# A decode step of cached attention and a gated MLP: part of one weight block by a transfer of its own, and scratch products ahead of half the V tiles

## The chip, the cores and the metric

The kernel runs on one core of a Trainium2 chip. That core has TensorE (PE, with its weight loads as PEld), VectorE (DVE), ScalarE (ACT), GpSimd (POOL) and SyncE (SP), and sixteen DMA engines that the queues of SP and ACT share. The metric is the device time of one execution in microseconds; the lower the better. All data are fp32.

## The reference

Eight tokens (B = 8) of width D = 512, one new position each. With xn = layernorm(x), the result is x + s * silu(y):

```python
q = (xn @ wq)                       # 32 heads of 128, grouped on 8 KV heads (REP = 4)
scores = q . k_cache * 128**-0.5    # cache of 4096 positions per token and KV head
s = softmax(scores) . v_cache @ wo  # wo is 4096 x 512
z = gelu(xn @ w_in)                 # 512 x 1792
z1, z2 = z[..., :896], layernorm(z[..., 896:])
y = (z1 * (w_sp * z2 + b_sp)) @ w_out   # w_out is 896 x 512
```

The K and V caches are 134 MB each, wq and wo 8.4 MB each, w_in and w_out 5.5 MB together; each byte is read once.

## The kernel before

Three SBUF slots of 64 KB per partition (`slot_a`, `slot_b`, `slot_c`; 8.4 MB each) take everything that is read. All transfers but the output's are issued from SP, in program order. In `prologue`, wq goes to slot b, then x, then the MLP's rows `w_mlp` to slot c (per partition: w_in, w_out as NB = 7 blocks of 128 rows, and a few scalars), then the first K tile to slot a. When q has been computed, the second K tile goes to slot b.

The MLP is computed in the prologue too. Its activations lie in four row groups of 32 partitions (`G` = 4, `R` = 32), 256 features in each of the first three and 128 in the last; they are transposed to `hT`, and the loop at L207 to L211 multiplies them with the seven blocks of w_out. Blocks 2g and 2g + 1 add up in row group g of the PSUM tile `pw`; block 6, the last, is alone in row group 3.

Then come eight KV heads, one after the other, each with four tiles: K for tokens 0 to 3 (slot a), K for tokens 4 to 7 (slot b), V for tokens 0 to 3 (slot c), V for tokens 4 to 7 (slot b). `Heads.loads` is SP's program: each transfer waits on PE's count for the products that free its slot. `head_products` is PE's program, one body that a loop on PE's own sequencer runs eight times; DVE and ACT have theirs written out (`head_sides`). PE waits for a tile's landing (`landed_a`, `landed_b`, `landed_c`) and for tokens from DVE (`take`), so its instructions stand in a fixed order: scores from both K tiles (L353), three small products for the softmax over row groups (L357 to L361), products of `pT` with the first V tile into `o_ps[0]` and with the second into `o_ps[1]` (L372), then two small products into `po` (L382), with two scratch products between them (L379) whose result nobody reads.

After the last head, `last_products` multiplies the heads' outputs with wo, which SP loads in six pieces into slot a (`WO_PIECES`; column 2m and 2m + 1 belong to product m). Products 0 to 27 are folded (L408, into `sc` and `o_ps`, copied out by DVE and ACT, and added up by `pick`, L430); products 28 to 31 go directly to `acc` (L417), two of them before L430 and two behind it. The last piece of wo holds one column. `last_sides` multiplies with the gate, adds x, and ACT stores the result.

Of the kernel before, what the change touches and what calls it, by code (L numbers as in the profile page):

```python
# [10 lines left out]
P = 128  # L11
B, D = 8, 512
HKV, REP, S, DH = 8, 4, 4096, 128
NK = D // P
G = 4
J = S // (G * P)
R = 32
FH = 896
FQ = 256
NB = FH // P  # L20
# [8 lines left out]
FOLDED = HKV * REP - REP  # L29
AHEAD = FOLDED + 2  # L30
HD = 256
N_IN, N_OUT = NK * 2 * FH, NB * D
N_MLP = N_IN + N_OUT + R
STEPS = 8
WARM = 384


class Chip:
# [49 lines left out]
        self.same_all = self.same.rearrange("p g r -> p (g r)")  # L88


def prologue(tc, t, x, w_mlp, wq, k0, k1, landed_a, landed_b):

    nc = tc.nc
    slot_a, slot_b, slot_c = t.slots
    nc.sync.dma_start(slot_b, wq)
    wq_sb = slot_b.rearrange("p (k n) -> p k n", k=NK)
    w_in_sb = slot_c[:, :N_IN].rearrange("p (k n) -> p k n", k=NK)
    w_out_sb = slot_c[:, N_IN:N_IN + N_OUT].rearrange("p (j d) -> p j d", j=NB)
    side_sb = slot_c[:, N_IN + N_OUT:N_MLP]
    x_sb = slot_c[:B, N_MLP + P:N_MLP + P + D]  # L100
    xn = slot_c[:B, N_MLP + P + D:N_MLP + P + 2 * D]
    nc.sync.dma_start(x_sb, x)
    nc.sync.dma_start(slot_c[:, :N_MLP], w_mlp)
    first = nc.sync.dma_start(slot_a, k0).then_inc(landed_a, 16)
    tc.no_tile_sem_insts.add(first.ins.name)

# [21 lines left out]
    def scratch(*shape):  # L128
        turn[0] ^= 1
        n = 1  # L130
        for s in shape[1:]:
            n *= s
        return t.scr[turn[0]][:shape[0], :n]
# [11 lines left out]
    for quad in range(HKV // G):  # L145
        pq = scratch(P, REP * DH)
        for k in range(NK):
            for g in range(G):
                lo = (quad * G + g) * REP * DH
                nc.tensor.matmul(pq[R * g:R * (g + 1), :], t.xnT[:, k, :], wq_sb[:, k, lo:lo + REP * DH],  # L150
                                 start=(k == 0), stop=(k == NK - 1))
# [12 lines left out]
    z, u_sb = zu[:, 0], zu[:, 1]  # L164
    rest = t.pT.rearrange("p j b g r -> p (j b g r)")
    hT, y_sb = rest[:, :2 * P].rearrange("p (a s) -> p a s", a=2), rest[:, D:]
# [36 lines left out]
    for a in range(2):  # L203
        th = scratch(P, P)
        nc.tensor.transpose(th, u_sb[:, 1, a * P:(a + 1) * P], t.ident)
        nc.vector.tensor_copy(hT[:, a, :], th)
    pw = scratch(P, D)  # L207
    for j in range(NB):
        g, a = divmod(j, 2)
        nc.tensor.matmul(pw[R * g:R * (g + 1), :], hT[:, a, R * g:R * (g + 1)], w_out_sb[:, j, :],  # L210
                         start=(a == 0), stop=(a == 1 or j == NB - 1))  # L211
    nc.vector.tensor_copy(y_sb, pw)
    py = scratch(P, W)
    for g in range(G):
# [3 lines left out]
    e = t.o_all.rearrange("p g d -> p (g d)")[:, :W]  # L218
# [9 lines left out]


class Heads:  # L230

# [109 lines left out]
    def head_products(self):  # L343
        nc, t, step = self.nc, self.t, lambda mm: mm.then_inc(self.pe, 1)
        slot_a, slot_b, slot_c = t.slots
        for half, (slot, landed) in enumerate(((slot_a, self.landed_a), (slot_b, self.landed_b))):
            self.take(landed, 16)
            k_sb = slot.rearrange("p (i c g s) -> p i c g s", i=HALF, c=2, g=G)
            for i in range(HALF):
                b = half * HALF + i  # L350
                for c in range(2):
                    for g in range(G):
                        mm = nc.tensor.matmul(t.sc[R * g:R * (g + 1), c, :], t.q[:, b * R:(b + 1) * R],  # L353
                                              k_sb[:, i, c, g, :], start=(b == 0), stop=(b == B - 1))
            step(mm)
        self.take(self.token, 1)
        step(nc.tensor.transpose(t.scr[0][:1, :P], t.nm, t.ident))  # L357
        self.take(self.token, 1)
        step(nc.tensor.transpose(t.scr[1][:, :1], t.full.rearrange("b g r -> b (g r)"), t.ident[:1, :1]))
        self.take(self.token, 1)  # L360
        step(nc.tensor.matmul(t.scr[1][:, 1:2], t.same_all, t.wl, start=True, stop=True))  # L361
        self.take(self.token, 1)
        pT = t.pT.rearrange("p j b g r -> p j b (g r)")
        for half, (slot, landed) in enumerate(((slot_c, self.landed_c), (slot_b, self.landed_b))):
            if half:
                self.take(self.token, 1)
            self.take(landed, 16)
            v_sb = slot.rearrange("p (i j e) -> p i j e", i=HALF, j=J)
            of = t.o_ps[half].rearrange("p g d -> p (g d)")
            for j in range(J):  # L370
                for i in range(HALF):
                    mm = nc.tensor.matmul(of[R * i:R * i + G * REP, :], pT[:, j, half * HALF + i],  # L372
                                          v_sb[:, i, j], start=(j == 0), stop=(j == J - 1))
            step(mm)
        n = HALF * REP
        for half in range(2):
            if half:
                for _ in range(2):
                    nc.tensor.matmul(t.scr[1][:, :WARM], t.ident, pT.rearrange("p j b x -> p (j b x)")[:, :WARM],  # L379
                                     start=True, stop=True)  # L380
            self.take(self.token, 1)
            mm = nc.tensor.matmul(t.po[:, half * n:(half + 1) * n], t.o_sb[half],  # L382
                                  t.fold.rearrange("p i r -> p (i r)"), start=True, stop=True)
        step(mm)
# [53 lines left out]
        step(mm)  # L438


def gqa_gmlp_decode(nc, x, kT, v, wq, wo, w_mlp, x_rows, out):
    t = Chip(nc)
    landed_a, landed_b, stored = (nc.alloc_semaphore(s) for s in ("landed_a", "landed_b", "stored"))
    with tile.TileContext(nc) as tc:
        prologue(tc, t, x, w_mlp, wq, kT[0, 0], kT[0, 1], landed_a, landed_b)
    heads = Heads(nc, t, landed_a, landed_b, stored)
    heads.loads(kT, v, wo, x_rows)
    for h in range(HKV):
        heads.head_sides(h)
    heads.last_sides(out)  # L450
    nc.sync.wait_ge(stored, 16).then_inc(stored, -16)
    with nc.tensor.Fori(0, HKV):
        heads.head_products()
    heads.last_products()
# [39 lines left out]
```

## Time and profile before

| what | us |
|---|---|
| median of 3 runs (lowest to highest) | 678.75 (678.7 to 679.01) |
| profiled execution, its own time | 679.39 |
| its span, first to last instruction | 678.1 |
| PE busy | 351.0 |
| PE weight loads busy | 102.7 |
| DVE busy | 80.7 |
| mean granted clock of PE | 0.748 |
| data queue of SP: bytes, share of sixteen engines | 290.79 MB, 99.1% |

Busy time is the time in which an engine worked on anything; a group of instructions is given by its line, its engine and the tiles it writes and reads. A matmul of fp32 data shows as two records. The granted clock is the share of TensorE's full clock that the chip allowed. The time ahead of an instruction in which its engine did nothing is given with what ended it. "PEq" is PE's own sequencer, which carries out PE's waits for landings and tokens, so that a wait for a transfer reads as a wait on PEq.

### The profile page before, as it was taken

How to read it: one execution, taken by the hardware profiler on the slowest of the kernel's cores; microseconds unless marked ns; L12 is line 12 of the kernel's file. 1: busy time of each engine (PE TensorE's matmuls, PEld its weight loads, DVE VectorE, ACT ScalarE, POOL GpSimd, SP SyncE). 2: the span in 40 equal slices, each digit the busy share in tenths (PEclk: the TensorE clock that was granted, in tenths of full speed). 3: DMA queues.
4: the chain of work that ended last, by engine and by line, in shares of the span. 5: the costliest groups of instructions: out<-in, count | busy, mean ns of one | idle time of the engine just before them, and what ended most of it. 6: DMA issues, size and time to landing. Idle time of an engine off the chain costs nothing. (4 is left out here: it accounts for less than half of the span.)

```text
span 678.1 us, 5431 instructions
## 1 busy us (share of the span) xinstructions
PE 351.0 (52%) x2480; PEld 102.7 (15%) x2480; DVE 80.7 (12%) x156; ACT 13.8 (2%) x28; POOL 2.8 (0%) x15
## 2 busy tenths in 40 slices
PE   0446743545565444456555444655645454655548
PEld 0112210111121111111111110111111111211104
DVE  0142021102110021101100021101101021100111
ACT  0010000000000000000000000000000000000000
POOL 1000000000000000000000000000000000000000
PEclk9986766778767677877766677887666678877659
DMA  9999999999999999999999999999999999999996
GB/s 383 439 433 434 434 433 433 434 433 433 433 433 433 433 433 433 437 437 437 445 437 433 437 437 433 441 437 433 433 433 433 433 433 433 433 433 433 433 414 287
DMA packets 6070, 290.90 MB, mean 429 GB/s; under 512 B 936, under 2 KB 1064, under 8 KB 1456
## 3 DMA queue, kind: packets, MB, share of 16 engines
q1 hardware_dynamic: 5920, 290.79, 99.1%
q8 instruction: 4, 0.07, 0.0%
q10 hardware_dynamic: 144, 0.03, 0.0%
q14 instruction: 2, 0.02, 0.0%
HBM read 290.78 MB, written 0.03 MB: 429 GB/s over the span
## 5 line engine op out<-in xcount | busy, mean ns | idle before, releaser
L372 PE MATMUL o_ps<-slot_b,pT 128*16 128x512 f32 x512 | 74.9, 751 | 81.0 <-PEq L341 81.0
L353 PE MATMUL sc<-slot_b,q 128*32 128x512 f32 x512 | 74.4, 746 | 73.5 <-PEq L341 73.5
L353 PE MATMUL sc<-slot_a,q 128*32 128x512 f32 x512 | 75.5, 756 | 56.2 <-PEq L341 56.2
L372 PE MATMUL o_ps<-slot_c,pT 128*16 128x512 f32 x512 | 73.9, 742 | 47.9 <-PEq L341 47.9
L258 DVE TENSOR_REDUCE nm<-sc 128x1 f32<-128x1024 f32 x8 | 9.8, 1225 | 277.0 <-PE sc L353 277.0
L258 DVE TENSOR_TENSOR o_all<-o_ps,diag 128x512 f32<-128x512 f32 x16 | 11.1, 692 | 243.4 <-PE o_ps L372 243.4
L353 PEld LDWEIGHTS sc<-slot_b,q 128*32 128x32 f32 x512 | 20.4, 134 | 127.5 <-issue 127.5
L372 PEld LDWEIGHTS o_ps<-slot_b,pT 128*16 128x16 f32 x512 | 17.6, 114 | 138.4 <-issue 138.4
L353 PEld LDWEIGHTS sc<-slot_a,q 128*32 128x32 f32 x512 | 20.7, 135 | 104.7 <-issue 104.7
L372 PEld LDWEIGHTS o_ps<-slot_c,pT 128*16 128x16 f32 x512 | 17.4, 114 | 97.7 <-issue 97.7
L289 ACT ACTIVATE p<-sc,nm 128x1024 f32<-128x1024 f32 x8 | 8.9, 1114 | 554.4 <-DVE nm L258 554.4
L258 DVE TENSOR_REDUCE o_sb<-o_all 128x128 f32<-128x512 f32 x16 | 16.4, 1025 | 0.5
L142 PE MATMUL scr<-ident,slot_c 8*128 8x8 f32 x4 | 0.6, 255 | 25.2 <-DVE slot_c L139 25.2
L379 PE MATMUL scr<-pT,ident 128*128 128x384 f32 x32 | 12.3, 507 | 0.0
L258 DVE STREAM_TRANSPOSE pT<-p 128x1024 f32<-128x1024 f32 x8 | 10.0, 1245 | 0.3
L150 PE MATMUL scr<-slot_b,xnT 128*32 128x512 f32 x64 | 9.0, 717 | 0.3 <-DVE xnT L143 0.3
L357 PE MATMUL scr<-ident,nm 128*1 128x128 f32 x8 | 2.2, 269 | 11.9 <-PEq L341 11.9
L382 PE MATMUL po<-fold,o_sb 128*128 128x16 f32 x32 | 6.1, 266 | 2.5 <-PEq L341 2.5
L361 PE MATMUL scr<-wl,same 128*128 128x1 f32 x16 | 3.6, 297 | 6.6 <-PEq L341 6.6
L382 PEld LDWEIGHTS po<-fold,o_sb 128*128 128x128 f32 x32 | 4.8, 188 | 14.0 <-issue 14.0
L258 DVE TENSOR_SCALAR p<-p,w,wl 128x1024 f32<-128x1024 f32 x8 | 6.5, 813 | 0.3
L379 PEld LDWEIGHTS scr<-pT,ident 128*128 128x128 f32 x32 | 5.5, 191 | 2.1
(92 smaller groups left out, 77.9 us busy)
## 6 DMA issues: line engine op xcount, KB each, us to landing
slot_c<-in_w_mlp SPq DMA_DIRECT2D x1, 5392.0 KB, 33.8
slot_a<-in_wo SPq DMA_DIRECT2D x1, 4608.0 KB, 40.1
slot_a<-in_wo SPq DMA_DIRECT2D x1, 2048.0 KB, 44.5
slot_a<-in_wo SPq DMA_DIRECT2D x2, 512.0 KB, 45.7
slot_a<-in_wo SPq DMA_DIRECT2D x1, 384.0 KB, 46.7
slot_a<-in_kT SPq DMA_DIRECT2D x8, 48.1
slot_b<-in_kT SPq DMA_DIRECT2D x8, 29.2
slot_c<-in_v SPq DMA_DIRECT2D x8, 48.1
```

The lines of the kernel that those rows point to most:

```text
L142: nc.tensor.transpose(pt[:, k * B:(k + 1) * B], xn[:, k * P:(k + 1) * P], t.ident[:B, :B])
L150: nc.tensor.matmul(pq[R * g:R * (g + 1), :], t.xnT[:, k, :], wq_sb[:, k, lo:lo + REP * DH], start=(k == 0), stop=(k == NK - 1))
L258: make(*args, **kw).then_inc(self.dve, 1)
L289: nc.scalar.activation(p, t.sc.rearrange("p c s -> p (c s)"), AF.Exp, bias=t.nm, accum_out=t.l).then_inc(self.act, 1)
L353: mm = nc.tensor.matmul(t.sc[R * g:R * (g + 1), c, :], t.q[:, b * R:(b + 1) * R], k_sb[:, i, c, g, :], start=(b == 0), stop=(b == B - 1))
L357: step(nc.tensor.transpose(t.scr[0][:1, :P], t.nm, t.ident))
L361: step(nc.tensor.matmul(t.scr[1][:, 1:2], t.same_all, t.wl, start=True, stop=True))
L372: mm = nc.tensor.matmul(of[R * i:R * i + G * REP, :], pT[:, j, half * HALF + i], v_sb[:, i, j], start=(j == 0), stop=(j == J - 1))
L379: nc.tensor.matmul(t.scr[1][:, :WARM], t.ident, pT.rearrange("p j b x -> p (j b x)")[:, :WARM], start=True, stop=True)
L382: mm = nc.tensor.matmul(t.po[:, half * n:(half + 1) * n], t.o_sb[half], t.fold.rearrange("p i r -> p (i r)"), start=True, stop=True)
```

## The change

Two parts.

First, w_out's last block. Its 128 rows no longer lie in the MLP's rows as one more block. Rows 64 to 127 are folded: their two halves of 256 columns lie on partitions 0 to 63 and 64 to 127, so that each MLP row gets 256 numbers (1,024 bytes) shorter. Rows 0 to 63 come by a transfer of their own, `w_lane`: five groups of 13 rows of 2,048 bytes (65 rows, the last of them zeros; in memory each group is followed by a row that is not read, so that five is an axis of its own). In the computation, the one product with block 6 becomes three: one of 512 columns over 64 rows, and two of 256 columns with operands `h_half`, in which half of the rows are zero. For `h_half` there is one more transpose, a memset and two copies.

Second, in every head, PE computes nine scratch products of 128 x 512 (identity times part of `pT`, into the scratch bank, read by nobody) behind the first V tile's products and ahead of the wait for the second V tile. They are a loop on PE's sequencer inside the loop over heads.

```diff
+WHOLE = NB - 1
+LANES, ROWS = 5, 13
+N_IN, N_OUT = NK * 2 * FH, WHOLE * D + D // 2
+AHEAD_OF_V = 9
...
     nc.sync.dma_start(slot_c[:, :N_MLP], w_mlp)
+    spare = N_MLP + P + 2 * D
+    w_lane_sb = slot_c[:LANES * ROWS, spare:spare + D]
+    h_half = slot_c[:, spare + D:spare + D + 2 * R].rearrange("p (e s) -> p e s", e=2)
+    nc.sync.dma_start(w_lane_sb, w_lane[:, :ROWS])
     first = nc.sync.dma_start(slot_a, k0).then_inc(landed_a, 16)
...
+    last_rows, low, high = slice((G - 1) * R, P), slice(0, P // 2), slice(P // 2, P)
+    tl = scratch(P // 2, R)
+    nc.tensor.transpose(tl, u_sb[last_rows, 1, P // 2:P], t.ident[last_rows, last_rows])
+    nc.vector.memset(h_half, 0.0)
+    nc.vector.tensor_copy(h_half[low, 0], tl)
+    nc.vector.tensor_copy(h_half[high, 1], hT[high, 0, last_rows])
     pw = scratch(P, D)
-    for j in range(NB):
+    for j in range(WHOLE):
         g, a = divmod(j, 2)
         nc.tensor.matmul(pw[R * g:R * (g + 1), :], hT[:, a, R * g:R * (g + 1)], w_out_sb[:, j, :],
-                         start=(a == 0), stop=(a == 1 or j == NB - 1))
+                         start=(a == 0), stop=(a == 1))
+    pl = pw[last_rows, :]
+    nc.tensor.matmul(pl, hT[low, 0, last_rows], w_lane_sb[low, :], start=True, stop=False)
+    for e in range(2):
+        nc.tensor.matmul(pl[:, e * (D // 2):(e + 1) * (D // 2)], h_half[:, e], w_half_sb, start=False, stop=(e == 1))
...
         for half, (slot, landed) in enumerate(((slot_c, self.landed_c), (slot_b, self.landed_b))):
             if half:
+                flat = t.pT.rearrange("p j b g r -> p (j b g r)")
+                with nc.tensor.Fori(0, AHEAD_OF_V):
+                    nc.tensor.matmul(t.scr[1], t.ident, flat[:, :512], start=True, stop=True)
                 self.take(self.token, 1)
             self.take(landed, 16)
...
+    w_lane = np.zeros((LANES * ROWS, D), np.float32)
+    w_lane[:P // 2] = w_out[-1, :P // 2]
+    w_lane = np.pad(w_lane.reshape(LANES, ROWS, D), ((0, 0), (0, 1), (0, 0)))
```

How the instructions stand. On PE, in one head, before (from the softmax's last small product to the end of the loop over heads):

```order
L361 MATMUL scr<-wl,same 128x1
L372 MATMUL o_ps<-slot_c,pT 16x512 x32
L372 MATMUL o_ps<-slot_b,pT 16x512 x32
L382 MATMUL po<-fold,o_sb 128x16
L379 MATMUL scr<-pT,ident 128x384 x2
L382 MATMUL po<-fold,o_sb 128x16
```

And now (lines are those of the changed kernel):

```order
L381 MATMUL scr<-wl,same 128x1
L395 MATMUL o_ps<-slot_c,pT 16x512 x32
L387 UNCONDITIONAL_BRANCH
L388 MATMUL scr<-pT,ident 128x512
L387 REGISTER_ALU
L387 COMPARE_AND_BRANCH
L395 MATMUL o_ps<-slot_b,pT 16x512 x32
L405 MATMUL po<-fold,o_sb 128x16
L402 MATMUL scr<-pT,ident 128x384 x2
L405 MATMUL po<-fold,o_sb 128x16
```

One product and its loop's branches stand between the two V tiles' products; the product is run nine times in each of eight heads.

On SP, the prologue's transfers, before:

```order
L95 DMA slot_b<-in_wq 128x16384
L102 DMA slot_c<-in_x 8x512
L103 DMA slot_c<-in_w_mlp 128x10784
L104 DMA slot_a<-in_kT 128x16384
L160 DMA slot_b<-in_kT 128x16384
```

And now:

```order
L98 DMA slot_b<-in_wq 128x16384
L106 DMA slot_c<-in_x 8x512
L107 DMA slot_c<-in_w_mlp 128x10528
L111 DMA slot_c<-in_w_lane 65x1x512
L112 DMA slot_a<-in_kT 128x16384
L168 DMA slot_b<-in_kT 128x16384
```

The MLP's rows are 256 numbers shorter, and a transfer of 65 rows stands between them and the first K tile.

More of the change, by code (lines that the diff above doesn't have):

```diff
@@ L31 @@
 HD = 256
-N_IN, N_OUT = NK * 2 * FH, NB * D
+WHOLE = NB - 1
+LANES, ROWS = 5, 13
+N_IN, N_OUT = NK * 2 * FH, WHOLE * D + D // 2
 N_MLP = N_IN + N_OUT + R
@@ L88, in __init__, with prologue @@
         self.same_all = self.same.rearrange("p g r -> p (g r)")
-def prologue(tc, t, x, w_mlp, wq, k0, k1, landed_a, landed_b):
+def prologue(tc, t, x, w_mlp, w_lane, wq, k0, k1, landed_a, landed_b):
     nc = tc.nc
@@ L97, in prologue @@
     w_in_sb = slot_c[:, :N_IN].rearrange("p (k n) -> p k n", k=NK)
-    w_out_sb = slot_c[:, N_IN:N_IN + N_OUT].rearrange("p (j d) -> p j d", j=NB)
+    w_out_sb = slot_c[:, N_IN:N_IN + WHOLE * D].rearrange("p (j d) -> p j d", j=WHOLE)
+    w_half_sb = slot_c[:, N_IN + WHOLE * D:N_IN + N_OUT]
     side_sb = slot_c[:, N_IN + N_OUT:N_MLP]
@@ L438, in last_products, with gqa_gmlp_decode @@
         step(mm)
-def gqa_gmlp_decode(nc, x, kT, v, wq, wo, w_mlp, x_rows, out):
+def gqa_gmlp_decode(nc, x, kT, v, wq, wo, w_mlp, w_lane, x_rows, out):
     t = Chip(nc)
@@ L444, in gqa_gmlp_decode @@
     with tile.TileContext(nc) as tc:
-        prologue(tc, t, x, w_mlp, wq, kT[0, 0], kT[0, 1], landed_a, landed_b)
+        prologue(tc, t, x, w_mlp, w_lane, wq, kT[0, 0], kT[0, 1], landed_a, landed_b)
     heads = Heads(nc, t, landed_a, landed_b, stored)
@@ L481 @@
             c(B_w_in).reshape(NK, P, 2 * FH).transpose(1, 0, 2).reshape(P, NK * 2 * FH),
-            w_out.transpose(1, 0, 2).reshape(P, NB * D),
+            w_out[:-1].transpose(1, 0, 2).reshape(P, WHOLE * D),
+            w_out[-1, P // 2:].reshape(P // 2, 2, D // 2).transpose(1, 0, 2).reshape(P, D // 2),
             side], axis=1),
+        "w_lane": w_lane,
         "x_rows": x_rows.reshape(P, W),
```

## The prediction

> **What bounds the kernel now.** I read the page first, for the transfers, then busy time by stretch, then the tail.
>
> ```profile
> span 678.1 us, 5431 instructions
> DMA  9999999999999999999999999999999999999996
> q1 hardware_dynamic: 5920, 290.79, 99.1%
> ```
>
> The DMA engines are busy from end to end: 290.79 MB on one queue fill 99.1% of sixteen engines' span. What TensorE (PE) does in mid-kernel costs no time. By stretch (columns: length, busy time of each engine with counts, granted clock, DMA share, GB/s):
>
> ```profile
> 75.00:575.00 500.00, 260.89 (x1740) 73.43 (x1740) 54.58 (x95) 9.86 (x21) 0.00 (x0) 0.73 1.00 434
> 672.50:673.00 0.50, 0.50 (x14) 0.21 (x6) 0.00 (x0) 0.00 (x0) 0.00 (x0) 1.00 0.53 176
> 673.00:673.50 0.50, 0.50 (x14) 0.25 (x10) 0.00 (x0) 0.00 (x0) 0.00 (x0) 1.00 0.32 113
> 673.50:674.00 0.50, 0.50 (x16) 0.30 (x10) 0.00 (x0) 0.00 (x0) 0.00 (x0) 1.00 0.29 90
> 674.00:674.50 0.50, 0.50 (x30) 0.39 (x27) 0.17 (x1) 0.11 (x1) 0.00 (x0) 1.00 0.14 35
> ```
>
> At 434 GB/s one engine of sixteen moves 27.1 GB/s. The engines do not end together. From 673.0 on the share is 0.32 of sixteen, that is five engines; the other eleven ran dry near 672.7, the five go on to about 674.3, some 1.5 us longer. The likely reason is in the queue rows: code comes in over the same engines. The first row is the whole run's, the second that of 672 to 675 us:
>
> ```profile
> q8 instruction: 4, 0.07, 0.0%
> q8 instruction: 1, 0.02, 1.8%
> ```
>
> Four blocks of some 16 KB and two smaller ones, each on some engine, hold up that engine's data. No view names single engines. Following the packets by hand, each starting where its engine's last one ended, I find the fetches on five engines; the transfer of x uses eight engines, and only one of the five late ones is among these eight.
>
> The tail, in order of time (start, length, engine, line; in brackets the idle time before):
>
> ```profile
> 636.02 9.32 PE L372 MATMUL o_ps<-slot_c,pT 128*16 128x512 f32 x64 [6.64 <-PEq L341]
> 655.32 9.91 PE L372 MATMUL o_ps<-slot_b,pT 128*16 128x512 f32 x64 [9.98 <-PEq L341]
> 665.41 1.54 PE L379 MATMUL scr<-pT,ident 128*128 128x384 f32 x4
> 667.64 0.62 PE L408 MATMUL sc<-slot_a,oT 128*8 128x256 f32 x8
> 673.91 0.38 PE L408 MATMUL o_ps<-slot_a,oT 128*8 128x256 f32 x1
> 674.39 0.37 ACT L330 COPY part_sb<-o_ps 128x256 f32<-128x256 f32 x1 [45.76 <-PE o_ps L408]
> 675.12 0.42 PE L430 MATMUL acc<-part_sb,pick 128*16 128x64 f32 x16 [0.38 <-PEq L341]
> 675.34 0.64 PE L417 MATMUL acc<-slot_a,oT_last 128*16 128x64 f32 x32
> 676.04 0.23 DVE L258 TENSOR_TENSOR gate<-acc,gate 128x64 f32<-128x64 f32 x1 [1.28 <-PE acc L417]
> ```
>
> PE runs without a break from 667.64 to 674.29: the folded products with wo (L408), the copies, `pick` (L430), the last direct products (L417). The weights they use arrive as follows (issue times, then KB and us from issue to landing; the six issues start 0.475 us apart):
>
> ```profile
> 625.90 2.80 SPq L279 DMA_DIRECT2D slot_a<-in_wo  x6
> slot_a<-in_wo SPq DMA_DIRECT2D x1, 4608.0 KB, 40.1
> slot_a<-in_wo SPq DMA_DIRECT2D x1, 2048.0 KB, 44.5
> slot_a<-in_wo SPq DMA_DIRECT2D x1, 384.0 KB, 46.7
> slot_a<-in_wo SPq DMA_DIRECT2D x1, 128.0 KB, 46.4
> ```
>
> So the first piece lands at 666.0, the second at 626.4 + 44.5 = 670.9, the fifth at 627.8 + 46.7 = 674.5, the sixth at 628.3 + 46.4 = 674.7. The last L417 group needs the fifth piece, and starts at 675.34, 0.8 us after it. In this execution the last 0.7 us thus belong to PE's chain, which started when the last V tile arrived (655.32); behind it, closely, stands the landing of wo.
>
> **The change, part by part.**
>
> *Fewer MLP bytes per row.* Each of the 128 rows gets 1,024 bytes shorter; an engine carries eight rows, 8,192 B, which at 27.1 GB/s is 0.30 us. Every later landing on an engine outside the five groups moves up by 0.30 us.
>
> *The transfer of five groups.* 65 rows of 2,048 B in five groups of 13. If each group goes to one engine, that engine gets 26,624 B, 0.98 us, less 0.30: it ends 0.68 us later. An early engine has 1.5 us to give, so it stays ahead of the late five. Bounds: all 65 rows on one engine would be 4.9 us there, spread over sixteen 0.3 us. I take five, as the access pattern is cut. The Trainium skill (DMA: Bandwidth & Descriptors, "Why a DMA increments its semaphore by 16 and not by 1") says that a transfer runs on the largest number of engines up to 16 that divides both slowest dimensions, the lowest-numbered ones; by it 5 and 65 give five engines, and they lie inside the eight of x. No view of this case shows it yet. [...]
>
> *Prologue work.* One more transpose, a memset, two small copies, and three products for one. The rows it resembles, and its cover:
>
> ```profile
> 53.73 0.50 DVE L206 COPY pT<-scr 128x128 f32<-128x128 f32 x2 [0.63 <-PE scr L205]
> 54.07 3.43 PE L210 MATMUL scr<-slot_c,pT 128*32 128x512 f32 x14 [0.17 <-DVE pT L206]
> 75.41 9.75 PE L353 MATMUL sc<-slot_b,q 128*32 128x512 f32 x64 [4.02 <-PEq L341]
> ```
>
> Seven products took 3.43 us, so two more are 1 us, at worst 1.7 us one after another; with copies and a transpose below 1 us together, 3 us at most. Everything behind waits for the second K tile, before which PE idles 4.02 us, so this costs nothing; without that cover it would be up to 3 us on the scores, still hidden by the DMA queue, in which a whole tile is waiting. One more issue on SP ahead of the first K tile lies under the transfer of wq:
>
> ```profile
> slot_b<-in_wq SPq DMA_DIRECT2D x1, 21.9
> ```
>
> *Nine scratch products ahead of each second V tile.* They stand in PE's queue behind the first V tile's products (end 645.34) and ahead of two waits; the second tile's products are queued behind them. Clock and pace (the last two rows count o_ps alone):
>
> ```profile
> 644.00:647.46 3.46, 1.34 (x16) 0.12 (x4) 1.71 (x2) 0.00 (x0) 0.00 (x0) 1.00 0.83 360
> 647.46:654.29 6.83, 0.00 (x0) 0.00 (x0) 0.00 (x0) 0.00 (x0) 0.00 (x0) 0.50 0.94 408
> 655.32:661.11 5.79, 5.79 (x28) 1.30 (x32) 0.00 (x0) 0.00 (x0) 0.50 1.03 446
> 661.11:665.23 4.12, 4.12 (x40) 0.95 (x32) 0.00 (x0) 0.00 (x0) 1.00 0.94 404
> ```
>
> The clock is full when the first tile's products end, falls to half at 647.46 after a stretch that was 39% busy, and the second tile runs its first 5.79 us at half clock (0.207 us per record against 0.103). A scratch product: L379 took 1.54 us for two of 384 columns, 1.03 us scaled to 512, the upper end; the lower is two records at a quarter of the array's four-wide pace, 8 x 0.103 = 0.82 us. Nine take 7.4 to 9.2 us, and end at 652.8 to 654.6, before the tile (655.32 - 0.30 = 655.0). PE then idles 0.4 to 2.2 us; the clock should hold, and the tile takes 64 x 0.103 = 6.6, with its end some 6.9 us, instead of 9.91. PE would reach L408 3.3 us earlier, at 664.3. In seven of eight heads this buys nothing, as DMA is the bound.
>
> *The tail now.* What is late next is wo. Its first piece lands at 665.7. I add 0.1 us for a wait's release (bounds 0, and the 0.36 us from the ACT copy's end, 674.76, to L430). L408's 56 products go at 0.114 us each (667.64 to 673.91): 36 of them from 665.8 to 669.9; the other 20 from the second piece, 670.7, to 673.0, with the tail of the last 673.3. From L408's end to L430 it took 0.83 us (674.29 to 675.12), L430's head start is 0.22: 674.35. The fifth piece is there at 674.5 - 0.3 + 0.1 = 674.3 too. L417 ends at 675.0 instead of 675.98: 1.0 us less.
>
> **Against the median.** The sum is made on the profiled execution, 679.39 us (678.1 and 1.29 around it), giving 678.4. The runs' median is 678.75, 0.64 lower. One reason is in the page:
>
> ```profile
> L372 PE MATMUL o_ps<-slot_b,pT 128*16 128x512 f32 x64 | 9.9, 788 | 10.0 <-PEq L341 10.0
> L372 PE MATMUL o_ps<-slot_b,pT 128*16 128x512 f32 x512 | 74.9, 751 | 81.0 <-PEq L341 81.0
> ```
>
> The last V tile took 9.9 us here, the mean of eight heads is 74.9 / 8 = 9.36: where the clock's step falls varies. In a usual execution PE's chain ends 0.55 us earlier, at 675.43, and wo's landing allows 675.25. There the change buys 675.43 - 675.0 = 0.45 us. I predict 678.3 us.
>
> **Rivals.**
>
> *A. A late engine is among the five.* Then it ends 0.68 us later, not 0.30 earlier. If it is the last of all, wo's fifth piece lands at 675.2, L417 ends at 675.95, and a usual execution becomes 0.5 us slower, 679.25; if it ends 0.3 us before the last, 678.95. For it: one late engine lies among x's eight. Against it: three of these eight are outside the five. It decides once that engine's lag plus 0.68 passes the others' less 0.30.
>
> *B. The clock falls in the gap after the scratch products.* A gap of up to 2.2 us leaves a 3.4 us stretch no more than 36% busy, and 39% was too little at 647. Then only the 0.30 us of landing stay, for PE's chain too: 678.45.
>
> *C. The scratch products overrun the tile*, the slower side. From 645.34 to 655.0 are 9.7 us, and L408 can slip by 1.5 more, so it decides from 1.24 us a product. At half clock they take 1.64 to 2.06, 14.8 to 18.5 in all: the tile starts 5.1 to 8.8 us late, saves 3.0, and the kernel takes 681 to 685. Against it: the clock is full when they start. The Trainium skill (Runtime: NRT & Kernel Launch, "Instruction fetch mechanics") says that a taken branch out of a two-block window stalls on a fetch. As a mechanism here: 1.8% of sixteen engines over 3 us is 0.86 us a fetch, with nine turns 7.8 us more, the same overrun. The trace speaks against it: all eight turns of the long head loop, with four q8 blocks in the run.
>
> *D. The change does not do what it says*: the groups land on one engine, which ends 4.6 us later, 3.1 us past the others' old end: 681.7.
>
> **How the numbers follow.** Forecast 0.5 (678.3, its own range 677.6 to 678.7), A 0.28, B 0.12, C 0.06, D 0.04. A measurement of this kernel can tell about 0.2%, 1.36 us, from no change: 677.4 and 680.1. The forecast, A and B lie inside; beyond the lower bound lies the forecast's edge, where executions like the profiled one, with its 1.0 us, are the usual ones or more than five engines gain: 0.1. C and D are slower: 0.1. The range that holds 8 in 10 takes in A with its bounds: 677.5 to 679.4.
>
> **What would show it.** Five engines' stretch in the changed profile: DMA share 0.6 near 673, with five engines of an extra step between the early and the late. The last wo landing earlier by 0.3 us: right; later by 0.4 or more: A. The clock at 1.00 from the first V tile to the tail and the second V tile near 6.9 us: right; 9 us and more: B. PE idle before L408 and again before its last 20 products: wo is the bound. A second V tile that starts after 655.5 is C. It would be wrong as a whole if the DMA queue had gaps in mid-kernel.

## The result, and the profile after

| | before | changed |
|---|---|---|
| median, 23 executions each | 678.98 us | 680.61 us |
| lowest | 678.37 us | 679.66 us |
| ratio, 95% interval | | 1.0038 [1.0026, 1.0050] |

The changed kernel is slower by 0.38%; 678.3 us had been forecast, with a range up to 679.4. Three of its executions (755.9 to 777.5 us; in the profiled one, 774.82 us, the core reads 376 GB/s over the span) are left out of the ratio, as are fourteen at 690 to 778 us of e1, e2, e6, e13 and e14, the kernels below with five groups of 10 or 13 rows; no other kernel here had one. The other twenty fall in two lots: sixteen from 679.66 to 681.47, mean 680.36, and four from 685.5 to 686.7. The sixteen stand 1.38 us above the median of before. The four, 5.8 us above the sixteen, add 4/20 of that, 1.16 us, to the mean. So there are two losses of about equal size to explain.

The profile below is of a second run of the changed kernel (`e1_again`), whose profiled execution took 681.61 us. From its page, the span, the DMA slices and the data queue:

```profile
span 679.6 us, 5886 instructions
...
DMA  9999999999999999999999999999999999999996
...
q1 hardware_dynamic: 5990, 290.79, 99.0%
```

The bytes are the same to two decimals and the queue is as full: 131,072 bytes left the MLP's rows, 133,120 came by the new transfer. The busy time of engines by stretch (columns as in the prediction; DMA share and GB/s last):

```profile
75.00:575.00 500.00, 305.85 (x1865) 96.10 (x1866) 54.66 (x95) 9.86 (x21) 0.00 (x0) 0.78 1.00 434
672.50:673.00 0.50, 0.50 (x16) 0.24 (x11) 0.00 (x0) 0.00 (x0) 0.00 (x0) 1.00 0.92 324
673.00:673.50 0.50, 0.50 (x18) 0.26 (x10) 0.00 (x0) 0.00 (x0) 0.00 (x0) 1.00 0.56 211
673.50:674.00 0.50, 0.50 (x16) 0.31 (x12) 0.00 (x0) 0.00 (x0) 0.00 (x0) 1.00 0.54 191
674.00:674.50 0.50, 0.50 (x14) 0.24 (x7) 0.00 (x0) 0.00 (x0) 0.00 (x0) 1.00 0.29 92
674.50:675.00 0.50, 0.50 (x14) 0.23 (x9) 0.00 (x0) 0.00 (x0) 0.00 (x0) 1.00 0.06 25
675.00:676.00 1.00, 1.00 (x42) 0.70 (x36) 0.15 (x1) 0.09 (x1) 0.00 (x0) 1.00 0.05 16
```

In mid-kernel it reads 434 GB/s, as before. At the end the sixteen engines stop in three steps. Near 673.2 the share is 0.56, nine engines; by 674.5 it is 0.06, a single engine, and this one works on until after 675.5. Before, the last five were done by 674.5. What the single engine carries is the end of wo (issue of its six pieces on SP, one every 0.475 us; then KB and time to landing, the second to fourth and the sixth piece between them):

```profile
626.92 2.80 SPq L299 DMA_DIRECT2D slot_a<-in_wo  x6
slot_a<-in_wo SPq DMA_DIRECT2D x1, 2048.0 KB, 44.8
slot_a<-in_wo SPq DMA_DIRECT2D x1, 384.0 KB, 46.8
slot_a<-in_wo SPq DMA_DIRECT2D x1, 128.0 KB, 46.7
```

The fifth piece (384 KB) lands at 626.92 + 4 x 0.475 + 46.8 = 675.6, where it was 674.5 before. PE's tail, in order of time:

```profile
637.30 9.07 PE L395 MATMUL o_ps<-slot_c,pT 128*16 128x512 f32 x64 [6.90 <-PEq L361]
646.30 7.99 PE L388 MATMUL scr<-pT,ident 128*128 128x512 f32 x18
656.62 7.06 PE L395 MATMUL o_ps<-slot_b,pT 128*16 128x512 f32 x64 [2.33 <-PEq L361]
667.48 0.62 PE L431 MATMUL sc<-slot_a,oT 128*8 128x256 f32 x8 [1.42 <-PEq L361]
669.68 1.11 PE L431 MATMUL sc<-slot_a,oT 128*8 128x256 f32 x8
675.63 0.62 PE L440 MATMUL acc<-slot_a,oT_last 128*16 128x64 f32 x28
676.64 0.42 PE L453 MATMUL acc<-part_sb,pick 128*16 128x64 f32 x16 [0.38 <-PEq L361]
676.86 0.64 PE L440 MATMUL acc<-slot_a,oT_last 128*16 128x64 f32 x32
```

The scratch products (L388) do what was meant: the second V tile's products take 7.06 us instead of 9.91. PE then waits 1.42 us for wo. The direct products (L440) start at 675.63, the moment the fifth piece is there, and the last ends at 677.50, 1.52 us later than before (675.98). The clock on the way:

```profile
646.30:654.29 7.99, 7.99 (x22) 3.33 (x18) 1.74 (x2) 0.00 (x0) 0.00 (x0) 1.00 0.87 378
654.29:656.62 2.33, 0.01 (x1) 0.04 (x2) 0.00 (x0) 0.00 (x0) 0.00 (x0) 1.00 1.10 475
656.62:663.68 7.06, 7.06 (x65) 2.03 (x65) 0.00 (x0) 0.00 (x0) 0.00 (x0) 1.00 0.97 418
666.00:668.00 2.00, 0.58 (x13) 0.35 (x16) 0.29 (x2) 0.00 (x0) 0.00 (x0) 1.00 0.95 410
669.00:672.00 3.00, 3.00 (x36) 1.35 (x30) 0.00 (x0) 0.00 (x0) 0.00 (x0) 0.50 0.97 398
```

It holds at 1.00 through the second V tile, and falls to half for 3.4 microseconds in the products with wo: the stall that the scratch products removed has moved to the wait for wo, and the clock fell there.

### The profile page after: what moved, and what is told of

Read it like the earlier page. It is cut to its first block, busy times and chain, and to the rows that moved or that the text cites. A ratio compares the mean times of both kernels' runs of the same rounds, so it can differ in the third digit from the quotient of the medians.

```text
span 773.2 us, 5886 instructions
## 1 busy us (share of the span) xinstructions
PE 412.6 (53%) x2629; PEld 129.6 (17%) x2629; DVE 81.3 (11%) x159; ACT 13.8 (2%) x28; POOL 2.8 (0%) x15
## 5 line engine op out<-in xcount | busy, mean ns | idle before, releaser
L373 PE MATMUL sc<-slot_b,q 128*32 128x512 f32 x512 | 72.2, 728 | 98.0 <-PEq L361 98.0
L395 PE MATMUL o_ps<-slot_c,pT 128*16 128x512 f32 x512 | 76.0, 760 | 76.0 <-PEq L361 76.0
L395 PE MATMUL o_ps<-slot_b,pT 128*16 128x512 f32 x512 | 72.0, 725 | 37.4 <-PEq L361 37.4
L388 PE MATMUL scr<-pT,ident 128*128 128x512 f32 x144 | 63.9, 598 | 0.0
L388 PEld LDWEIGHTS scr<-pT,ident 128*128 128x128 f32 x144 | 26.7, 190 | 37.4 <-issue 37.4
```

The lines of the kernel that those rows point to most:

```text
L388: nc.tensor.matmul(t.scr[1], t.ident, flat[:, :512], start=True, stop=True)
```

## The experiments

Theory A is rival A of the prediction: the engine that ends last is among the five, and every row that it is given puts off the last landing of wo. Theory P came late: five engines that run about half a 64 KB packet behind the others make all reads slower. All ratios are to the kernel before, run on the same chip. Landing times given per engine, and the length of single packets, are read from the trace's own records of landings and packets; no view shows them.

### The two halves alone

The changed kernel a second time:

> The changed kernel once more, for a profile beside those of its parts. Both theories: 680 to 681 us. Theory L (the lanes: five DMA engines that run 1 us behind the others disturb the reads of all) expects a rate under 434 GB/s in mid-kernel. Theory S (the scratch products: PE's inner loop delays PE, or its own code fetches, and with it the tail) expects 434 GB/s in mid-kernel and a last V tile that starts late.

1.0032 [1.0014, 1.0050]; its compared executions took 679.75, 680.12, 681.61 and 683.43 us. The landings of wo's sixth piece come at 672.9 to 673.2 on seven engines, at 674.1 to 674.7 on eight, and at 675.97 on one. The new transfer's own semaphore rises five times, so it does run on five engines.

The block's split and transfer, without the scratch products:

```diff
-                flat = t.pT.rearrange("p j b g r -> p (j b g r)")
-                with nc.tensor.Fori(0, AHEAD_OF_V):
-                    nc.tensor.matmul(t.scr[1], t.ident, flat[:, :512], start=True, stop=True)
```

> The changed block of w_out alone, no scratch products. Theory L: all of the loss is here, 680 to 681 us, mid-kernel rate under 434 GB/s. Theory S: 678.4 to 679.3 us, by rival A or the forecast's DMA term, 434 GB/s.

1.0042 [1.0019, 1.0065]; seven executions lie from 679.81 to 680.72, two at 686.25 and 686.65. This part alone brings the whole loss, both lots of it. By stretch:

```profile
673.00:673.50 0.50, 0.50 (x16) 0.26 (x11) 0.00 (x0) 0.00 (x0) 0.00 (x0) 1.00 0.59 228
675.00:675.50 0.50, 0.50 (x28) 0.39 (x23) 0.01 (x1) 0.00 (x0) 0.00 (x0) 1.00 0.06 25
675.50:676.00 0.50, 0.39 (x27) 0.22 (x14) 0.41 (x1) 0.37 (x1) 0.00 (x0) 1.00 0.07 23
```

Nine engines at 673, a single one from 675 to 676, as in the whole change.

The scratch products alone, on the kernel before:

```diff
+AHEAD_OF_V = 9
...
             if half:
+                flat = t.pT.rearrange("p j b g r -> p (j b g r)")
+                with nc.tensor.Fori(0, AHEAD_OF_V):
+                    nc.tensor.matmul(t.scr[1], t.ident, flat[:, :512], start=True, stop=True)
                 self.take(self.token, 1)
```

> The nine scratch products alone. Theory L: not slower than before, 678.3 to 679.0 us, and the second V tile takes 6.9 us. Theory S: all of the loss is here, 680 us or more, and the last V tile starts more than 0.3 us after its landing.

1.0021 [0.9998, 1.0045]: ten executions from 678.64 to 680.89 and one at 688.31. No gain, and a spread that before does not have (678.44 to 679.48). The execution at 688.31 had a mean granted clock of 0.629, the other ten 0.796 to 0.811. In the profiled one (678.81 us) the gap behind the scratch products cost the clock:

```profile
644.50 7.99 PE L369 MATMUL scr<-pT,ident 128*128 128x512 f32 x18
655.36 8.76 PE L376 MATMUL o_ps<-slot_b,pT 128*16 128x512 f32 x64 [2.87 <-PEq L342]
655.36:659.50 4.14, 4.14 (x24) 1.14 (x28) 0.00 (x0) 0.00 (x0) 0.00 (x0) 0.59 0.99 427
659.50:664.10 4.60, 4.60 (x45) 1.24 (x37) 0.00 (x0) 0.00 (x0) 0.00 (x0) 1.00 0.91 393
```

After 2.87 us of idleness the clock is mostly at half up to 659.5: rival B, in this execution. The sixth piece of wo lands at 674.75, against 674.68 before, so the scratch products do not move the transfers.

### How many engines, how many rows

Here the scratch loop is out, and only the cut of the transfer changes. If theory A holds, the loss must follow the rows per engine, and vanish when each of sixteen engines gets four (the 8 KB that its shorter MLP rows saved).

```diff
-LANES, ROWS = 5, 13
+LANES, ROWS = 16, 4      # e4_spread16
+LANES, ROWS = 4, 16      # e5_lanes4
+LANES, ROWS = 8, 8       # e9_lanes8
+LANES, ROWS = 5, 25      # e10_rows25: 61 of the 125 rows are zeros
```

> As e2_lanes, but the 64 rows come in sixteen groups of four, so that each of sixteen engines carries as many bytes as before. Theory L: 678.7 to 679.2 us, as before, since no engine is set back against the others. Theory S: the same, as there are no scratch products. If it is at 680 us or more, the cause is neither the lag nor the scratch products, but the extra transfer itself, its 2 KB rows or the prologue's added work.

> As e2_lanes, but four groups of 16 rows instead of five of 13. Theory A (rival A: one of the five engines that take the groups is itself a late one, so the last landing moves back by about 1.3 us): if that engine is the fifth, wo's last landing comes 0.3 us earlier than before and the time is 678.4 to 678.7 us; if it is one of the first four, each takes 32 KB instead of 26 KB and the time is 680.2 to 681 us, 0.2 above e2_lanes. Theory N (no engine is special; the extra small rows slow all): 680 to 681 us with five or more engines late at the end together.

> As e2_lanes, but eight groups of 8 rows: eight engines carry 16 KB each. Theory A (the engine that fetches DVE's code is among those that take groups, and ends last): the last landing goes with the rows on that engine; 13 rows moved it by +1.3 us, so a row costs 0.12 us with the 0.30 us taken off once, and 8 rows give +0.65: 679.5 us. Theory N (not the rows on one engine but an extra transfer cut finer than sixteen): 680.5 us as e2_lanes.

> As e2_lanes, but five groups of 25 rows, 12 of them idle zeros: the five engines are set back by about one whole 64 KB packet (2.42 us) instead of half of one. Theory A: +2.7 us on the last landing, 681.5 us. Theory P (where the values lie more than 1.5 us above the lowest of a kernel, the reads of two groups of engines half a packet apart disturb each other): the values keep within 1.5 us. Without P: scattered upward as e2_lanes.

| run | rows per engine | sixth piece of wo, last landing | executions, us | ratio |
|---|---|---|---|---|
| before | 0 | 674.68 | 678.4 to 680.2 | |
| e4_spread16 | 4 | 674.79 | 678.70 to 679.86 (11) | 1.0006 [0.9997, 1.0015] |
| e9_lanes8 | 8 | 675.23 | 679.10 to 680.46 (10) | 1.0010 [1.0001, 1.0019] |
| e1, e2 | 13 | 675.97, 676.31 | see above | 1.0032, 1.0042 |
| e5_lanes4 | 16 | 676.47 | 680.33 to 682.70 (6) | 1.0034 [1.0022, 1.0046] |
| e10_rows25 | 25 | 677.57 | 681.40 to 681.81 (5) | 1.0039 [1.0026, 1.0052] |

The landing follows the rows, and with it the time. From e4's 674.79 to e10's 677.57 it is 2.78 us for 21 rows, 0.13 us a row. The ends of the DMA show it, first e4's and then e10's:

```profile
674.00:674.50 0.50, 0.43 (x32) 0.28 (x24) 0.00 (x0) 0.00 (x0) 0.00 (x0) 1.00 0.23 72
674.50:675.00 0.50, 0.50 (x44) 0.50 (x39) 0.00 (x0) 0.00 (x0) 0.00 (x0) 1.00 0.02 5
```

```profile
675.50:676.00 0.50, 0.50 (x16) 0.24 (x8) 0.00 (x0) 0.00 (x0) 0.00 (x0) 1.00 0.12 37
676.50:677.00 0.50, 0.50 (x32) 0.36 (x29) 0.29 (x1) 0.30 (x1) 0.00 (x0) 1.00 0.06 25
```

With four rows each the last engine is done by about 674.6; with 25 on five of them one engine alone still reads at 676.5 to 677. The same split of the block, with all its extra products in the prologue, costs at most 0.15% when its rows are spread: the prologue's work is not the loss.

### The rows without their use, and which engine is late

An idle transfer of zeros, five groups of seven rows, on the kernel before; nothing reads it:

```diff
     nc.sync.dma_start(slot_c[:, :N_MLP], w_mlp)
+    spare = N_MLP + P + 2 * D
+    nc.sync.dma_start(slot_c[:5 * 7, spare:spare + D], idle[:, :7])
```

> The kernel before, and one transfer of five groups of 7 rows of zeros that nothing uses; w_out's block stays in the MLP's rows. Theory A: the last landing +0.84 us (7 rows at 0.12), 679.7 us, with no change to anything that is computed. If it is as before, 678.9 us, the loss of e2_lanes comes from the computation or the MLP's rows.

1.0032 [1.0008, 1.0056]: ten executions from 679.07 to 681.21, median of all 679.64, and two at 686.63 and 687.39. The last landing is at 675.36. The transfer alone, with no work behind it, brings both lots of the loss.

Three small transfers, whose packets differ in length, mark the engines:

```diff
+    for n, cols in ((4, 448), (3, 384), (2, 320)):
+        nc.sync.dma_start(slot_c[:n, spare:spare + cols], idle[:n, :cols])
+        spare += D
```

> The kernel before, with three small transfers of 4, 3 and 2 rows of different lengths that nothing uses: the lengths of the packets tell which of the engines carries which. Theory A expects the engine that ends last, with DVE's code blocks, among the first four, so that it has a packet of the 4-row transfer. Time within 0.2 us of before.

678.57 us, one execution. On one engine a packet starts 3 or 4 ns before the recorded end of the one before it, so that engines can be followed. The engine that twice fetches 8 KB of code (q14 in the page; at 95.2 and 559.7 us) leads back to a group of five that run within 5 ns of one another: one of them has a packet of the transfer of four rows and none of the other two, four have no marked packet at all. With four groups (e5) the engine of the 8 KB blocks carries rows of the transfer, so it is among the first four, if a transfer of n rows takes the first n; in e12 that leaves the one with the packet of the four-row transfer, the fourth engine. The blocks of 16 KB (q8) at 44.3, 80.5 and 119.1 us go to engines that carry none of the marked packets. So the fourth engine is one that every transfer of five groups loads; in e11 it carries seven of the idle rows. That it is the fourth is read from one execution each of e12 and e5.

### The clock in the wait for wo

Two more scratch products stand ahead of the products with wo, so that PE does not idle there. In `e6_filler` they are added to the changed kernel; in `e8_scratch_filler` the block's split is out, and eleven products instead of nine close the gap ahead of the V tile too; `e7_lanes4_full` has all of it with four groups of sixteen rows.

```diff
+AHEAD_OF_WO = 2
...
+        flat = t.pT.rearrange("p j b g r -> p (j b g r)")
+        for _ in range(AHEAD_OF_WO):
+            nc.tensor.matmul(t.scr[1], t.ident, flat[:, :512], start=True, stop=True)
```

> The whole change, and two more scratch products once, between the last head and the products with wo, while PE waits for wo's first piece. Theory C (the clock falls to half in that wait and the folded products then run slow, as in e1_again): the clock stays at 1.00 through the folded products and the values over 679.9 us go; median 679.8. Rival: the clock has no part, the landing alone sets the end: as e1_again, 680 to 681.5 us.

1.0048 [1.0025, 1.0071], from 679.83 to 686.48: the upward lot covers what the filler may give, and the run decides nothing.

> Four groups instead of five, eleven scratch products ahead of each second V tile instead of nine, and the two ahead of wo. Theory A with the fifth engine the late one: 678.0 to 678.4 us, below before. With one of the first four: 680 us.

1.0025 [1.0015, 1.0035], from 680.42 to 681.01. Beside e5 (680.33 to 682.70) the spread is smaller, the lowest time the same: PE's work can't give what the late engine holds (last landing 677.01 here).

> No groups: eleven scratch products ahead of each second V tile and the two ahead of wo. Theory C: PE's chain is out of the way in every run, and the landing of wo sets the end: 678.5 us, with the values from 679 to 681 of e3_scratch gone. Rival: the inner loop itself costs time at random: 679.4 us as e3_scratch.

0.9995 [0.9986, 1.0003], eleven executions from 678.53 to 678.95. The values of e3 at 679 to 681 are gone. Its tail:

```profile
644.74 9.71 PE L370 MATMUL scr<-pT,ident 128*128 128x512 f32 x22
655.38 7.06 PE L377 MATMUL o_ps<-slot_b,pT 128*16 128x512 f32 x64 [0.93 <-PEq L343]
664.74 1.98 PE L407 MATMUL scr<-pT,ident 128*128 128x512 f32 x4
666.64 0.62 PE L416 MATMUL sc<-slot_a,oT 128*8 128x256 f32 x8
665.00:672.00 7.00, 7.00 (x94) 2.96 (x97) 0.15 (x2) 0.00 (x0) 0.00 (x0) 1.00 0.98 409
```

PE is busy throughout and the clock stays at 1.00 from 665 to 672, where e1 had lost it. So the spread that the scratch products alone brought goes with the falls of the clock in the waits that they opened. Which wait did it in e3's slow executions is inferred from e1, since e3's one profile shows the other gap. With both gaps closed PE is early, and the time is still that of before: the landing of wo is the floor.

### The executions 6 us higher

Left over are the values near 686 us in every kernel with five groups of 7 or 13 rows, which 0.13 us a row does not give. They were absent with 4, 8 and 16 groups (14, 10 and 11 executions) and with 25 rows on five (5 executions). Three idle transfers ask whether the lag of the five decides:

```diff
+    nc.sync.dma_start(slot_c[:5 * 10, spare:spare + D], idle[:, :10])   # e13; 13 rows in e14, 18 in e15
```

> The kernel before, and behind w_mlp an idle transfer of five groups of ten rows of zeros (2 KB a row, 20 KB per engine); nothing else changes. Theory A (the extra rows on the engine that ends last cost 0.10 to 0.12 us each in the last landing of wo): 679.9 to 680.1, all executions within 0.5 us of each other. Theory P (five engines that run about half of a 64 KB packet, 1.2 us, behind the others make every read slower): the same middle, but one execution in five or more lies 4 us or more above it; a profile of such an execution shows packets of more than 2.45 us from end to end. An all-over rise of the middle to 682 would speak for P alone.

> As before, with five groups of thirteen idle rows, the numbers of the changed kernel's transfer, but w_mlp keeps its length and the prologue its work. Theory A: 680.2 to 680.5, all within 0.5 us. Theory P: five engines 1.3 us behind; one execution in five or more lies 4 us or more above the middle. If neither scatter nor a higher middle shows, the scatter of the changed kernel does not come from the transfer's size alone.

> As before, with five groups of eighteen idle rows, 36 KB per engine. Theory A: 680.7 to 681.1, all within 0.5 us. Theory P: the five engines are 1.9 us behind, four fifths of a packet and no longer half: no scatter, 680.7 to 681.1 as well. Scatter here too would say that any transfer on five engines brings it, whatever its size (against it stands the run with five groups of 25 rows, without scatter).

| run | ratio | compared executions, us |
|---|---|---|
| e13_idle10 | 1.0031 [1.0015, 1.0047] | seven from 679.77 to 680.36, then 682.50, 685.41 |
| e14_idle13 | 1.0062 [1.0034, 1.0090] | five from 679.91 to 681.28, then 683.13, 685.56, 686.18, 687.73, 689.14 |
| e15_idle18 | 1.0033 [1.0020, 1.0046] | 680.81 to 681.58, and 683.06 (the profiled one; its span is 680.9, those of the others 679.5 to 680.0) |

Scatter at 10 and 13 rows, none of 4 us or more at 18, in five executions: as theory P said. The lower values of 10 and 13 rows are those of theory A; those of 18 lie up to 0.5 us above its figure, on the side of 0.13 us a row. And the profiled execution of e14, at 686.18 us, is one of the high ones. From 38 to 84 us and from 90 to 670 us in e14, with the landing of the second K tile and of the first V tile (us from issue):

```profile
38.00:84.00 46.00, 21.50 (x147) 7.12 (x143) 9.31 (x23) 2.17 (x3) 0.56 (x1) 0.70 1.00 388
90.00:670.00 580.00, 293.38 (x2007) 82.95 (x2000) 62.47 (x108) 11.26 (x24) 0.00 (x0) 0.74 1.00 434
slot_b<-in_kT SPq DMA_DIRECT2D x1, 44.7
slot_c<-in_v SPq DMA_DIRECT2D x1, 40.2
```

The same rows in e13's execution, at 680.36 us:

```profile
38.00:84.00 46.00, 27.15 (x188) 8.85 (x192) 9.58 (x24) 2.17 (x3) 0.56 (x1) 0.74 1.00 431
90.00:670.00 580.00, 302.48 (x2044) 85.45 (x2048) 61.97 (x106) 9.86 (x21) 0.00 (x0) 0.73 1.00 433
slot_b<-in_kT SPq DMA_DIRECT2D x1, 39.2
slot_c<-in_v SPq DMA_DIRECT2D x1, 33.9
```

The engines are always busy (share 1.00), but for 46 us they read 388 GB/s instead of 431: 46 x 43/431 = 4.6 us late, and as late from then on. Single packets say the same. Starts (us) and lengths (ns) of the sixteen 64 KB packets near 37 to 40 us:

```
e14   eleven start 37.76 to 38.33, five start 39.01 to 39.20: 2714 to 2716 each
e13   eleven start 37.25 to 37.89, five start 38.32 to 38.83: 2418 to 2424 each
e15   eleven start 38.30 to 38.79, five start 39.79 to 40.06: 2418 to 2424 each
e1    eleven start 37.20 to 37.47, five start 38.40 to 38.54: 2418 to 2426; at 42 us 2500 to 2506; at 45 us 2418 to 2424 again
e2    eleven start 37.32 to 37.97, five start 38.46 to 38.94: 2418 to 2424, and 2418 still at 42 to 57 us
before: all sixteen within 0.47 us, 2418 each
```

In e14 the five start 1.1 us after the eleven (difference of the means), about half a packet, and all packets stay at 2.71 us until 84 us. In e1, with the same lag, the packets begin to stretch at 41 us; a code block that comes at 42.3 puts one engine out of step, and the stretch is gone. With a lag of 1.0 us (e13) or 1.5 (e15) it does not begin. But neither does it in e2, where the five are 1.1 us behind as well; and in e11, where they are only 0.5 us behind in the profiled execution, two of twelve executions are high. So the transfer on five engines brings the high executions (e11, e13 and e14 have nothing else), but that the lag of half a packet decides, as theory P has it, is not shown. Why the packets stretch in one execution and not in another, and what ended it at 84 us in e14, stays open.

## Why the prediction was wrong

**What bounds the kernel: right.** DMA stays at a share of 1.00 and the end follows wo's landing. The argument against the median was right too: in e8 PE's chain is out of the way, and that buys no time that can be measured, since usual executions were bound by the landing already.

**"An early engine has 1.5 us to give, so it stays ahead of the late five": the step that failed.** It holds for four of the five engines (674.1 to 674.3 in e1's sixth piece; the latest of all but one engine are at 674.7). The fifth is the last engine of all, the one of the 8 KB code blocks: at 620 us of e1 it runs 1.7 to 1.8 us behind the other four. The prediction had found one late engine among x's eight, and gave this case 0.28, weighing that three of the eight are outside. Two of the late engines carry a packet of x: the one of the 8 KB blocks in e11, and in e12 that of the 16 KB block at 119.1 us. The Trainium skill (DMA: Bandwidth & Descriptors, "Why a DMA increments its semaphore by 16 and not by 1") says that such a transfer uses the lowest-numbered engines, the greatest number up to 16 that divides both slowest dimensions. The five landings in e1 agree, and e12's packets fit "lowest-numbered".

**"Every later landing on an engine outside the five groups moves up by 0.30 us": wrong too.** The MLP's rows themselves did land earlier, at 34.63 to 35.08 us in e1 against 34.86 to 35.39 before. But while the five engines carry their rows, the next 64 KB packets of the other eleven take 2.90 to 3.01 us instead of 2.42, and the 0.30 is lost: these engines end wo's sixth piece no earlier than before (from 672.94, against 672.70), and the latest engine outside the five is at 674.68, where the last one of before was. So even without the late engine among the five there was nothing to gain at the landing.

**Rival A was the right mechanism, with too low a price.** It put the fifth piece at 675.2; it came at 675.63. Two terms were off: the 0.30 us above, and the row. A 2 KB row was priced by the rate, 0.98 us for 13, 0.075 each. In the trace of e1 the 65 row packets take 0.084 to 0.184 us, 0.112 in the mean, 1.45 us for 13; and the next 64 KB packets of the five engines take 2.64 to 2.75 us, 0.27 more than 2.42. That is 1.72 us, 0.13 a row. The same sum is 0.35 + 0.34 us for e4's four rows and 3.23 + 0.28 for e10's 25: 2.82 us between the two, where the last landings stand 2.78 apart.

**The scratch products: right in themselves.** Predicted 7.4 to 9.2 us for nine, a gap of 0.4 to 2.2 us, a tile of 6.9 us at full clock; measured 7.99, 2.33 (just above) and 7.06. Rival C is out: they end 2.33 us before the tile. Its rule from the Trainium skill (Runtime: NRT & Kernel Launch, "Instruction fetch mechanics") shows nowhere here: the nine turns run without a gap, 0.89 us each.

**The tail after them: wrong in one thing.** That PE waits for wo was foreseen ("PE idle before L408"), that the clock falls in that wait was not. Rival B named the mechanism at the other gap, where e3's execution had it. The Trainium skill (TensorE: Matmul & The Clock Gate, "What's actually happening") has activity judged in windows of some 3.4 us; the half clock of e1, between the wait and full work, lasts 3.41 us (668.70 to 672.11), and that of e3 3.41 us too.

**The prologue's work costs nothing: right**, by e4, and by e14 beside e2: its lowest value, without that work, is 679.91, e2's 679.81.

**The upward executions** were no case of the prediction, and are half of the mean loss. Nothing in the profile of before shows them, as its engines start within 0.47 us of one another and not in two groups. Rival D (one engine for all groups) did not occur.

## What to carry to other kernels

When the DMA engines are full from end to end, the time is that of the engine that ends last; before giving bytes to a few engines, find out whether that one is among them, and let each engine carry the same. A small transfer on a few engines can also slow all the reads for a while, in some executions only, so time such a change many times. And a filler ahead of one wait is worth nothing if the work behind it stops at the next transfer, where the clock may fall instead.

## What was not expected of the hardware

- Rows of 2 KB put off the end of a full queue by 0.13 us each (e4 to e10), against 0.075 by the rate of large packets: a row's packet took 0.112 us in the mean in e1, 0.129 in e10.
- While five engines carried such rows, the 64 KB packets of the other eleven took 2.90 to 3.01 us (13 rows, e1) and 3.51 to 3.63 us (25 rows, e10) instead of 2.42.
- Code comes over the data engines: two fetches of 8 KB in mid-kernel, at 95.2 and 559.7 us in e12, fall on the engine that ends last. Alone among the engines it ended 1.3 us after all others once it was given 13 rows more.
- With five engines 1.1 us behind eleven, a 64 KB packet took 2.71 us instead of 2.42 for some 46 us, at 388 instead of 431 GB/s, in the profiled execution of e14 and not in those of e2, e13 and e15.
